# Gate and up products of two chunks as 2x2 blocks by Strassen's method in a fused attention and SwiGLU kernel

## The chip, the cores and the metric

The kernel runs on one core of a Trainium2 chip. The metric is the device time of one execution in microseconds (us), lower is better. Engines are named as in the profile: PE (TensorE, the matrix multiplier, with PEld for its weight loads), DVE (VectorE), ACT (ScalarE), POOL (GpSimd) and SP (SyncE, which here issues transfers and passes semaphores on). SBUF is the on-chip memory that all of them work from; PSUM is the memory in which matmuls accumulate, in 8 banks of 128 x 512 numbers.

## What is computed

Two branches read the same x (2048 rows of 640) and are mixed by a gate per row. Branch A is attention over 4 segments of 512 rows with 32 heads of 20 columns, and a linear memory that each segment reads and adds to. Branch B is a SwiGLU network with 1728 hidden columns:

```python
def _B_ref(x, w1, w3, w2):
    gate = jnp.einsum("bsd,df->bsf", x, w1)
    up = jnp.einsum("bsd,df->bsf", x, w3)
    h = _silu(gate) * up
    out = jnp.einsum("bsf,fd->bsd", h, w2)
    return out

x = A_x
g = _sigmoid((x * gate_w).sum(-1, keepdims=True))
a = _A_ref(x, A_wq, A_wk, A_wv, A_wo, A_beta)
b = _B_ref(x, B_w1, B_w3, B_w2)
return g * a + (1 - g) * b
```

The change is in `gate` and `up`, and in what stands around them.

## The kernel before

**Tiling.** A segment of 512 rows of x is a chunk; chunks 0 and 1 are pair A, chunks 2 and 3 pair B. x lies transposed: 128 of its 640 columns on the partitions, 512 rows along them, so a chunk is five such k-blocks (KB = 5). The 1728 hidden columns are 13 tiles j of 128 and a half tile of 64 (NF = 13 is the number of the half tile, in which gate and up share one weight tile). Every fp32 operand of a projection is kept as two fp32r parts, high and low (`split`, L177-184: ACT rounds the high part, DVE or POOL subtracts to get the low one), and every product is three passes: high by high, high by low, low by high (`PASSES`).

**Two halves of PE.** A matmul over 128 rows of the array is issued as two of 64 rows, one on the upper and one on the lower half (`halves`, L219). The two halves run at the same time. A piece of such work is a `Work`: its upper matmuls go first, then, one bank later in the stream, its lower ones, so that in the order of the program the lower half of one Work stands between the upper matmuls of the next. The lower half of a Work may begin when the upper one's last matmul has been signalled through an SP no-op (L272).

**gate and up.** For each j and each chunk of the pair there is one Work for the gate and one for up (`proj`, `ffn_up`): 15 products of 512 columns, as 30 matmuls of 64 rows. A pair has 4 Works and 120 matmuls per j. Each W tile is split once and used for both chunks. When the gate is in its bank, ACT takes tanh(g/2) (L1043), DVE makes (tanh+1)*g (L1040) and then 0.5*that*up (L1057); the tile is stored to DRAM (`hd`), from which `ffn_down` (the tiles f) reads it for the product with w2.

**Order.** Everything is written out by a planner in the program itself, which keeps a clock for each half of PE (`clocks`) and an end of work for each engine (`busy`), and writes the instructions of all engines in one order. The hardware executes that order, each engine its own rows in turn, with semaphores for what one engine needs of another. The stream of heavy Works (q, k, v, g, u, f, op) comes from segments `segs`; attention units (s: scores for the row maximum, t: scores for the exponentials, o: probabilities by v) are put in at fixed slots, `side` streams (`braid`) at fixed distances. When nothing heavy can go on the upper half, the planner writes lower ones (`lower`), else it moves its clock on (`force`). Tiles come from rings: NW weight tiles W, NRAW raw weight tiles, NFT tiles f, NHT tiles hT, 8 PSUM banks, two large slots `acc` for x raw, v and the output accumulators.

**Places.** The up stage of pair A runs from 125 to 366 us of the profiled execution (g and u with attention units between); that of pair B is spread between 590 and 930 us, with k, q, v and op work between.

Of the kernel before, what the change touches and what calls it, by code (L numbers as in the profile page):

```python
# [29 lines left out]
NFT = 6  # L30
NST, NW, NRAW, NHT, NVG, NB, FREE = 4, 9, 4, 4, 2, 8, 2000
# [20 lines left out]
def gated_mix(ctx: ExitStack, tc: tile.TileContext, xT, wqk, wv, w13, w2, w2h, wo, beta, out):  # L52
# [10 lines left out]
    hd = [dp.tile([4, 3, P, D], F32, name=f"hd{c}") for c in range(NSEG)]  # L63
# [122 lines left out]
    class Work:  # L186

        def __init__(self, name, parts, evac, old=None, olds=None, ready=None, hooks=None):
            self.ready, self.hooks = ready, hooks or {}
            self.name, self.parts, self.evac, self.old, self.olds = name, parts, evac, old, olds or {}  # L190
# [70 lines left out]
    def one(r, w):  # L261
# [6 lines left out]
        else:  # L268
            ins = nc.tensor.matmul(o, l, x, start=i == 0 and (r == 0 or not w.todo[0]),  # L269
# [58 lines left out]
    def events():  # L328
# [13 lines left out]
        for d in list(sides):  # L342
            if not d.on:
                sides.remove(d)
            elif dense["ns"] >= d.due and len(under) < 2 and len(behind_one) < 3:
# [4 lines left out]
                elif isinstance(y, Work) and (y.ready is not None and not y.ready() or not free(3) or busy["dve"] > now() + 2000):  # L350
# [6 lines left out]
    on_step, units = [], deque()  # L357
# [19 lines left out]
    def step(run):  # L377
# [82 lines left out]
    def slot(name):  # L460
        return cp.tile([P, 4 * H * VE], F32, tag="acc", name=name, bufs=2)
# [10 lines left out]
    def w_add(src, n, queue=nc.sync, needs=(), even=False, home=None):  # L472
        items.append((src, n, queue, needs, even, home))
        return len(items) - 1
# [21 lines left out]
    def w_load():  # L496
# [17 lines left out]
        clock["next"] += 1  # L514

    def w_split():
# [11 lines left out]

        def done():
            tiles[k] = w  # L530
            halfway.remove(k)
            if k not in EARLY:
# [4 lines left out]
    halfway, homes = set(), {}  # L537

    def w_step():
# [5 lines left out]
        elif raws and raws[0][0] < limit() and now() >= raws[0][3]:  # L545
# [6 lines left out]
    def w_get(i):  # L552

        while i not in tiles:
            if i >= limit():
                if not lower():
                    set_oldest(min(w.old for w in under if w.old is not None))
                    if i >= limit():
                        raise RuntimeError("no room for weight " + str(i))
# [6 lines left out]
            elif not raws or raws[-1][0] < i and len(raws) < NRAW:  # L566
# [208 lines left out]
    def q_block(c, mb, i, alloc, oldest=None, then=None):  # L775
# [7 lines left out]
        yield Work(f"q{c}_{mb}", proj(i, Xs[c]), evac, i if oldest is None else oldest, then and {3 * KB - 1: then})  # L783
# [76 lines left out]
    def v_blocks(c, iv, end):  # L860
# [3 lines left out]
        def begin_v():  # L864
            big["v", c] = V = slot(f"V{c}").rearrange("p (l h e) -> p l h e", l=4, e=VE)
# [915 lines left out]
```

## Time and profile before

| | |
|---|---|
| median of 3 runs | 1088.2 us (1087.52 to 1088.9) |
| the profiled execution | 1088.77 us, its span 1087.1 us |
| PE busy | 1073.8 us, 99% of the span, 11681 matmuls |
| DVE, ACT, POOL busy | 581.7, 483.5, 513.3 us (54%, 44%, 47%) |
| granted clock of PE | 0.998 of full speed |
| transfers | 184.36 MB, mean 170 GB/s |

The profile is one execution. A group row gives a line, an engine, an operation, the tiles written and read, the count, the busy time and the mean length of one instruction. The length of a matmul runs from its start until its result is through, so matmuls overlap and their lengths are not their spacing; spacing is read from the starts in the timeline. A busy share says only that some matmul is under way: with two halves of the array, PE is "busy" also when one half has nothing to do.

### The profile page before, as it was taken

What the parts mean: (1) busy time and instruction counts of PE and PEld (TensorE: products, weight loads), DVE (VectorE), ACT (ScalarE), POOL (GpSimd) and SP (SyncE); (2) the same over time, 40 slices, a digit from 0 to 9 for tenths busy, and PEclk for the clock granted to TensorE, in tenths of its full rate; (3) what the DMA queues carried; (4) which work ended last, traced back from release to release, by engine and by line L of the source; (5) the groups of instructions that cost most, each with busy time, mean ns of one, the idle gap of its engine ahead of it and who ended that gap; (6) DMA issues with size and microseconds to landing.
All of it is one profiled execution on the core that took longest, in us unless ns stands there. A gap on an engine that the chain in (4) does not pass through costs nothing.

```text
span 1087.1 us, 29863 instructions
## 1 busy us (share of the span) xinstructions
PE 1073.8 (99%) x11681; PEld 966.5 (89%) x11681; DVE 581.7 (54%) x1717; ACT 483.5 (44%) x1003; POOL 513.3 (47%) x718
## 2 busy tenths in 40 slices
PE   9999999999999999999999999999999999999998
PEld 7999998987877999899988889898888888899898
DVE  6022475444455676474544666774445665564553
ACT  6255324333333574353755653444333434565220
POOL 4543434353533446447564545647444543454250
PEclk9999999999999999999999999999999999999999
DMA  8465764444555555656776786655546463563541
GB/s 324 149 215 210 240 185 127 132 124 115 141 131 144 139 161 154 181 154 178 234 243 183 253 292 198 190 142 182 151 117 168 143 159 108 153 169 115 165 163 50
DMA packets 124645, 184.36 MB, mean 170 GB/s; under 512 B 21356, under 2 KB 65304, under 8 KB 124504
## 3 DMA queue, kind: packets, MB, share of 16 engines
q1 hardware_dynamic: 93064, 126.25, 37.1%
q0 software_dynamic: 23664, 42.04, 15.5%
q10 hardware_dynamic: 7776, 14.16, 3.5%
q8 instruction: 93, 1.52, 0.6%
q14 instruction: 48, 0.39, 0.1%
HBM read 112.23 MB, written 69.21 MB: 167 GB/s over the span
## 4 chain that ended last, share of the span: by engine, by line
PE 92%; DMA 3%; POOL 1%; issue 1%; DVE 1%; ACT 1%; SPq 0%; POOLq 0%; DVEq 0%
PE g L269 17%; PE f L269 17%; PE u L269 15%; PE k L269 7%; PE v L269 7%; PE op L269 6%; PE o L1275 6%; PE q L269 5%; PE s L1180 4%; PE t L1242 4%; PE q L806 1%; PE pm L269 1%; DMA qk<-qkd 1%; PE nd L269 1%; DMA qk<-mr 1%
## 5 line engine op out<-in xcount | busy, mean ns | idle before, releaser
L269 PE MATMUL g<-X,W 64*128 64x512 f32 x1680 | 377.1, 394 | 0.0
L269 PE MATMUL u<-X,W 64*128 64x512 f32 x1560 | 351.9, 394 | 0.0
L1191 DVE CUSTOM_DVE_ANT_0 junk<-s,mask 128x128 bf16<-128x128 f32 (+3 forms) x512 | 251.2, 491 | 161.7 <-PE s L1180 122.1
L179 POOL TENSOR_TENSOR W<-wr,W 128x640 fp32r<-128x640 f32 (+2 forms) x133 | 206.5, 1557 | 177.2 <-ACT W L184 165.7
L269 PEld LDWEIGHTS g<-X,W 64*128 64x128 f32 x1680 | 259.5, 185 | 16.1 <-issue 2.0
L1249 ACT ACTIVATE P<-t 128x384 f32<-128x384 f32 (+1 forms) x384 | 181.0, 525 | 179.9 <-PE t L1242 170.0
L269 PEld LDWEIGHTS u<-X,W 64*128 64x128 f32 x1560 | 244.4, 185 | 14.4 <-issue 1.2
L1258 POOL TENSOR_SCALAR_AFFINE_SELECT P<-P 128x256 f32<-128x256 f32 (+1 forms) x192 | 95.5, 504 | 263.6 <-ACT P L1249 237.7
L269 PE MATMUL f<-XW,W 64*128 64x320 f32 x1536 | 160.9, 310 | 3.6 <-SPq L272 3.6
L269 PEld LDWEIGHTS f<-XW,W 64*128 64x128 f32 x1536 | 153.8, 186 | 4.6 <-SPq L272 4.1
L184 ACT CAST W<-wr 128x640 fp32r<-128x640 f32 (+2 forms) x170 | 119.7, 719 | 54.8 <-PE u L269 19.3
L269 PE MATMUL f<-W,W 64*128 64x320 f32 x1056 | 138.6, 309 | 0.0
L269 PEld LDWEIGHTS f<-W,W 64*128 64x128 f32 x1056 | 118.8, 186 | 1.2 <-issue 1.0
L269 PE MATMUL k<-X,W 64*128 64x512 f32 x600 | 108.3, 398 | 0.0
L1180 PE MATMUL s<-qk 60*128 60x256 f32 (+2 forms) x512 | 91.0, 326 | 1.9 <-DMA qk<-qkd 1.8
L1242 PE MATMUL t<-qk 62*128 62x256 f32 (+2 forms) x512 | 88.2, 325 | 3.2 <-DMA qk<-mr 1.4
L269 PE MATMUL op<-W,oT 64*128 64x320 f32 x960 | 90.7, 308 | 0.0
L269 PE MATMUL v<-W,X 64*128 64x322 f32 (+2 forms) x948 | 89.2, 310 | 0.0
L269 PEld LDWEIGHTS k<-X,W 64*128 64x128 f32 x600 | 81.2, 185 | 6.2 <-issue 0.6
L269 PEld LDWEIGHTS op<-W,oT 64*128 64x128 f32 x960 | 85.8, 185 | 0.6 <-issue 0.4
L1201 POOL DMA_DIRECT2D qk<-mr x128 | 73.0, 572 | 28.1 <-DVE mr L1217 25.2
L269 PEld LDWEIGHTS v<-W,X 64*128 64x128 f32 (+1 forms) x948 | 84.8, 186 | 0.3 <-issue 0.2
(120 smaller groups left out, 1358.9 us busy)
## 6 DMA issues: line engine op xcount, KB each, us to landing
qk<-qkd POOLq DMA_DIRECT2D x128, 240.0 KB, 4.5
wr<-in_w_dram SPq DMA_DIRECT2D x80, 320.0 KB
hd<-ft SPq DMA_DIRECT2D x52, 256.0 KB
qkd<-qs SPq DMA_DIRECT2D x20, 512.0 KB
qkd<-ks SPq DMA_DIRECT2D x20, 512.0 KB
wr<-hd SPq DMA_DIRECT2D x32, 320.0 KB
od<-oq ACTq DMA_DIRECT2D x32, 256.0 KB
wr<-in_wo_dram SPq DMA_DIRECT2D x20, 320.0 KB
```

Source lines behind the costliest of these rows:

```text
L179: return lambda: e.tensor_sub(dst[:, 1], src, dst[:, 0].bitcast(F32))
L184: stages(bank, ("act", ns, lambda: nc.scalar.copy(dst[:, 0], src)), low, done=done)
L269: ins = nc.tensor.matmul(o, l, x, start=i == 0 and (r == 0 or not w.todo[0]), stop=i == len(todo) - 1 and (r == 1 or not w.todo[1]), skip_ ...
L806: nc.tensor.matmul(ps[m], ws[m][:, a, kb * P:(kb + 1) * P], Xs[c][:, b, kb, :], start=count[m] == 0, stop=count[m] == 14, skip_group_check ...
L1180: nc.tensor.matmul(ps[i][:, o:o + n], q[:, qb * P:(qb + 1) * P], k[:, :n], start=qb != 1, stop=qb != 0, skip_group_check=True)
L1191: nc.vector.tensor_tensor_reduce(out=junk[:, :n], in0=ps[i][:, o:o + n], in1=mask[:, L - n:], scale=1.0, scalar=-3.0e38, op0=ALU.add, op1= ...
L1201: nc.gpsimd.dma_start(dst, src)
L1242: nc.tensor.matmul(ps[i][:, o:o + L - q0], k[:, kb * P:(kb + 1) * P], q[:, q0:], start=kb != 2, stop=kb != 3, skip_group_check=True)
L1249: nc.scalar.activation(u["P"][:, i, o:o + n], ps[i][:, b:b + n], AF.Exp, scale=SCALE)
L1258: nc.gpsimd.affine_select(d, d, pattern=[[0, 2], [0, n], [1, P]], base=0, channel_multiplier=-1, compare_op=ALU.is_ge, fill=0.0)
L1275: nc.tensor.matmul(ps[32 * i:32 * i + 32, kb * P:], heads[2 * p + i]["v"][:, kb], pairs[p + i // 2]["P"][:, i % 2, o:o + n], start=kb == 0 ...
```

## The change

For each j the pair's gate and up are written as a 2x2 block product: rows are the two chunks, inner blocks are k-blocks (0, 1) and (2, 3), columns are gate and up. Seven block products replace eight (Winograd's form, with sums of x and sums of weights as operands); k-block 4 is done directly as before. Each block product is 2 k-blocks x 3 passes x 2 halves = 12 matmuls, so a j has 7 x 12 + 24 = 108 matmuls for 120.

- `make_sums` loads the two chunks' raw k-blocks 0 to 3 once more (8 loads of 256 KB a pair, tiles sx), makes four sums of each (DVE or POOL), and splits them into S tiles that lie in the `acc` slots, and into k-blocks 0 and 1 of the second chunk's X, which they overwrite.
- `mix` makes the sums of a j's two raw weight tiles: five subtractions on DVE or on POOL. A j has four W tiles (one of them 256 wide) for two. The ring of W goes from 9 to 8 tiles, that of f from 6 to 8, of hT from 4 to 3.
- `ffn_pair` replaces `ffn_up`. Its seven Works of a j are c1, c6, c7, c4 in one bank, z5, z3 in a second, w2 in a third. A later Work of a bank adds to what stands in it, after ACT or DVE has read it: c6 may begin when ACT has copied c1 to a tile (a), c7 when c6 is copied (b), c4 when c7 is copied (d), z3 when DVE has added z5 to d. Then follow adds of b and d on DVE, tanh on ACT, and two products on DVE or POOL. The Works of block j and block j-1 are interleaved: c1(j) c7(j-1) z5(j-1) w2(j) c6(j) c4(j-1) z3(j-1).
- The half tile has a Work of its own (`ffn_half`), once for each chunk. hidden tiles of a pair are stored in one transfer of 512 KB for two of 256 KB. The factor 0.5 moves to `cgate`.
- The segments are arranged anew: k, q of chunks 2 and 3 are no longer done together (7 more weight tiles of wqk), all of the second pair's up work comes after chunk 3's projections, and the ends of the segments move (slots 38, 70, 76, 105 of heads become 35, 61, 77, 104).
- Where no Work is ready and no event is due, the planner now lets its clock go on by a step in place of an error.

```diff
-NFT = 6
-NST, NW, NRAW, NHT, NVG, NB, FREE = 4, 9, 4, 4, 2, 8, 2000
+NFT = 8
+NST, NW, NRAW, NHT, NVG, NB, FREE = 4, 8, 4, 3, 2, 8, 2000
...
     def open_work(w):
-        w.bank = k = take_bank()
-        w.ps = pp.tile([P, L], F32, tag=f"b{k}", name=w.name, bufs=1)
+        w.more = bool(w.box)
+        if w.more:
+            w.bank, w.ps = w.box
+        else:
+            w.bank = k = take_bank()
+            w.ps = pp.tile([P, L], F32, tag=f"b{k}", name=w.name, bufs=1)
+            if w.box is not None:
+                w.box += [k, w.ps]
...
-                if not heap:
-                    raise RuntimeError("nothing makes " + waiting[0].name + " ready")
-                force()
+                if heap:
+                    force()
+                else:
...
+                    dense["ns"] += STEP
+                    clocks[:] = [c + STEP for c in clocks]
...
+    def mix(w, ri, rj, k, done):
...
+        def sums(v):
+            v.tensor_sub(ri[:, a], rj[:, a], ri[:, a])
+            v.tensor_sub(t, rj[:, b], ri[:, a])
+            v.tensor_sub(rj[:, a], rj[:, b], rj[:, a])
+            v.tensor_sub(ri[:, b], ri[:, b], t)
+            v.tensor_sub(ri[:, e], ri[:, e], rj[:, e])
+        stages(None, either(1650, 3200, sums), done=lambda: split(w[:, :, :2 * P], t, None, 300, done, spare=EVEN))
...
+            def run(v, x=x):
+                v.tensor_add(x[2], x[2], x[1])
+                v.tensor_sub(x[1], x[0], x[1])
+                v.tensor_sub(x[0], x[2], x[0])
+                v.tensor_sub(x[3], x[3], x[0])
+            stages(None, either(2500, 5100, run), done=left.clear)
...
+            return dict(
+                c1=lambda: work("c1", chain, [(wa, k, xs(x, k)) for k in range(2)], copy_to("a")),
+                w2=lambda: work("w2", w, [(wa, k, xs(x, k)) for k in (2, 3, 4)], evac_w, drop=wa),
+                c6=lambda: work("c6", chain, [(wd, k, ss(2, k)) for k in range(2)], copy_to("b"), ("a",), wd, (2,)),
+                c7=lambda: work("c7", chain, [(wb, k, ss(3, k)) for k in range(2)] + [(wb, 4, xs(y, 4))], copy_to("d"), ("b",), None, (3,)),
+                z5=lambda: work("z5", z, [(wc, k, ss(1, k)) for k in range(2)], evac_5, (), None, (1,)),
+                c4=lambda: work("c4", chain, [(wc, k, xs(y, k)) for k in (2, 3, 4)], evac_4, ("d",), wc),
+                z3=lambda: work("z3", z, [(wb, 2 + k, ss(4, k)) for k in range(2)] + [(wb, 4, xs(x, 4))], evac_3, ("5",), wb, (4,)))
+        for p in plan:
+            now_ = block(*p)
+            for n, b in (("c1", now_), ("c7", last), ("z5", last), ("w2", now_), ("c6", now_), ("c4", last), ("z3", last)):
+                if b is not None:
+                    yield b[n]()
+            last = now_
...
-    seg += [braid(chain(jobs_up(A, FIRST)), job_read(1), 3800, 11000)]
-    segs.append((H + LAG + 1, seg))
+    half = job_half(1)
+    up = job_pair(A)
+    seg = [braid(braid(chain(q + [half, up]), (0, make_sums(A)), 400, 0), job_read(1), 3800, 11000)]
+    segs.append((H + 3, seg))
...
-    ks = jobs_k_held(B)
-    seg += ks[:KSKIP] + [alternate(chain(ks[KSKIP:]), job_up(B, 0))]
-    segs.append((2 * H + 6, seg))
...
+    segs.append((2 * H - 3, seg))
+    ks = jobs_k((2,), range(2)) + job_q((2,), 2) + job_q2((2,), 3)
...
-    tail = [braid(chain([d1b, take(d2, 14)]), o1, 1400, 6000), o2, d2]
+    tail = [braid(chain([d1b, d2]), o1, 1400, 6000), o2]
```

In the order of the program the two rows of `gate` and `up` look like this at the start of pair A's up stage. On PE before, the gate Work g0_0 (upper half) stands between the lower matmuls of the q projection:

```order
L269 MATMUL g0_0_1871<-X0_104,W15_1039 128x512
L269 MATMUL q1_3_1780<-X1_106,W13_919 128x512
L269 MATMUL g0_0_1871<-X0_104,W15_1039 128x512
L269 MATMUL q1_3_1780<-X1_106,W13_919 128x512
L269 MATMUL g0_0_1871<-X0_104,W15_1039 128x512
L269 MATMUL q1_3_1780<-X1_106,W13_919 128x512
```

and now, on PE at the first block of pair A (g1_13 is the half tile of chunk 1, c10_0 the chain bank and w20_0 the bank of w2 of chunk pair 0, block 0; S0_0 is a tile of sums):

```order
L275 MATMUL g1_13_1894<-X1_104,W15_1054 128x512 x8
L275 MATMUL c10_0_1958<-X0_102,W16_1154 128x512 x4
L1390 MATMUL s1_1_0_2040<-qk1_89 128x384
L1390 MATMUL s1_1_1_2041<-qk1_89 128x384
L275 MATMUL c10_0_1958<-X0_102,W16_1154 128x512 x2
L275 MATMUL w20_0_1976<-X0_102,W16_1154 128x512 x4
L1390 MATMUL s1_2_0_2061<-qk1_89 128x512
L1390 MATMUL s1_2_1_2062<-qk1_89 128x512
L275 MATMUL w20_0_1976<-X0_102,W16_1154 128x512 x4
L275 MATMUL c10_0_1958<-S0_0_1799,W17_1327 128x512 x2
```

Where upper and lower alternated, the rows from g1_13 to w20_0 are all lower halves, 22 of them with only two s pairs between; the next upper one is c6, the last row, which reads S and adds to the bank of c1.

The second place is ACT in the middle of pair A's up stage. Before, exponentials P, casts of W and the tanh of a gate:

```order
L184 CAST W33_3272<-wr33_2877 128x640 [waits DMAHW4_49,PE_49]
L1280 COPY oq4_3325<-o4_3308 128x512 [waits DMAHW3_49,PE_49]
L716 DMA od0_76<-oq4_3325 128x512 [waits DMAHW6_49,Activation_49]
L1043 ACTIVATE ft0_5_3340<-g0_5_3182 128x512 [waits DMAHW5_49,PE_49]
L1249 ACTIVATE P6_3355<-t6_0_0_3356 128x512 [waits PE_49,Pool_49]
L1249 ACTIVATE P6_3355<-t6_0_1_3357 128x512 [waits PE_49]
L1249 ACTIVATE P6_3355<-t6_1_0_3412 128x384 [waits PE_49]
L1249 ACTIVATE P6_3355<-t6_1_1_3413 128x384 [waits PE_49]
L1043 ACTIVATE ft1_5_3455<-g1_5_3301 128x512 [waits PE_49]
```

and now, with the copies a and d (L1212) of blocks 8 and 7:

```order
L1459 ACTIVATE P8_3884<-t8_1_0_3946 128x384 [waits PE_49]
L1459 ACTIVATE P8_3884<-t8_1_1_3947 128x384 [waits PE_49]
L184 CAST W51_3969<-wr49_3544 128x640 [waits DMAHW0_49,Pool_49]
L1212 COPY a0_8_3990<-c10_8_3909 128x512 [waits PE_49]
L1459 ACTIVATE P8_3884<-t8_2_0_4012 128x384 [waits PE_49]
L1459 ACTIVATE P8_3884<-t8_2_1_4013 128x384 [waits PE_49]
L1212 COPY d0_7_4024<-c10_7_3660 128x512 [waits PE_49,Pool_49]
L184 CAST W52_4047<-wr52_3741 128x640 [waits DMAHW1_49]
L1459 ACTIVATE P9_4088<-t9_0_0_4089 128x512 [waits PE_49,Pool_49]
```

Each of the two copies stands behind a pair of exponentials, the first behind a cast of W as well; PE's Works c6 and c4 are behind these copies. Before, no later matmul stood behind a tanh of the up stage except through the bank it frees.

More of the change, by code (lines that the diff above doesn't have):

```diff
@@ L349, in events @@
                     sides.remove(d)
-                elif isinstance(y, Work) and (y.ready is not None and not y.ready() or not free(3) or busy["dve"] > now() + 2000):
+                elif isinstance(y, Work) and (y.ready is not None and not y.ready() or not free(2) or busy["dve"] > now() + 2000):
                     d.held = y
@@ L514, in w_load @@
         clock["next"] += 1
+        kind = items[k][6]
+        if kind is not None:
+            kind[1].append(raw)
+            if len(kind[1]) == 2:
+                for i in range(2):
+                    raws.append([k + 1 + i, kind[1][i], D, t + AGE])
+                clock["next"] += 2
     def w_split():
@@ L1138, in ffn_down @@
         for c, lb in hi:
-            if first and lb == 0:
-                accs[c] = slot(f"acc{c}")[:, :4 * D].rearrange("p (b d) -> p b d", b=4)
             for hf in range(2):
@@ L1391, in over @@
                 done()
-        while c not in turned:
+        while c not in turned or c == 1 and read.count(2) < 8:
             yield 1
```

298 lines of the change are left out of this document (215 added, 83 removed).

## Prediction

> **What bounds the kernel now.** I read the page first: engines, then the chain that ended last, then the costliest groups.
>
> ```profile
> PE 1073.8 (99%) x11681; PEld 966.5 (89%) x11681; DVE 581.7 (54%) x1717; ACT 483.5 (44%) x1003; POOL 513.3 (47%) x718
> ...
> PE 92%; DMA 3%; POOL 1%; issue 1%; DVE 1%; ACT 1%; SPq 0%; POOLq 0%; DVEq 0%
> ...
> L269 PE MATMUL g<-X,W 64*128 64x512 f32 x1680 | 377.1, 394 | 0.0
> L269 PE MATMUL u<-X,W 64*128 64x512 f32 x1560 | 351.9, 394 | 0.0
> ```
>
> PE is the bound: busy 99% of the span, 92% of the chain. So what counts is how long PE's rows take, and what PE waits for. The waits of PE alone, of which these are the longest, are small:
>
> ```profile
> PE f L269 <- SPq L272: 3.6, 2, 2.2
> PE s L1180 <- DMA qk<-qkd: 1.8, 3, 1.0
> PE t L1242 <- DMA qk<-mr: 1.4, 2, 1.0
> ```
>
> How long a row takes is seen in the timeline of PE, in three stretches: gate and up alternating on the two halves; f alternating; and the end of the kernel, where only one Work is left and its second half runs alone (start, length, matmuls).
>
> ```profile
> 204.06 0.39 PE L269 MATMUL u<-X,W 64*128 64x512 f32 x1
> 204.12 0.39 PE L269 MATMUL g<-X,W 64*128 64x512 f32 x1
> 204.29 0.39 PE L269 MATMUL u<-X,W 64*128 64x512 f32 x1
> 204.36 0.39 PE L269 MATMUL g<-X,W 64*128 64x512 f32 x1
> ...
> 393.45 3.48 PE L269 MATMUL f<-W,W 64*128 64x320 f32 x44
> ...
> 1081.51 1.93 PE L269 MATMUL f<-XW,W 64*128 64x320 f32 x12
> ```
>
> u and g start as good as together, and each comes again 0.23 us later. So a half takes a 512-wide matmul every 0.23 us, and two halves that both have work take one every 0.115. Of f (0.31 us long) 44 in a row span 3.48 us: (3.48-0.31)/43 = 0.074 each with both halves at work. The 12 at the end span 1.93 us: (1.93-0.31)/11 = 0.147 each, twice as much. **A matmul whose half works alone costs twice the PE time of a paired one**, and a busy share of 99% does not show it. That is the point on which this prediction turns.
>
> **The change part by part.**
>
> *Matmuls removed.* 12 of 120 for each of 13 j in two pairs: 12 x 26 = 312, as the program's order has it (3240 g and u become 2928). If all were paired, 312 x 0.115 = 35.9 us.
>
> *Pairing lost.* The planner pairs a Work's lower half with the next Work's upper half. g and u never waited for each other; the seven new Works do. c6 needs the copy of c1, c7 that of c6, c4 that of c7, z3 the add of z5, and each such copy comes only after the lower half of its Work is through. Where the next upper half may not begin yet, lower halves go alone: the 22 rows shown above are 21 such neighbours. A Work's rows are first all upper, then all lower ones, so neighbours on the same half can be counted in the order (the attention's own pairs left out). Before there are 422: 138 of 512 columns (q, k, g, u), 272 of 320 (v, f, op), 12 others. Now there are 773: 357, 405 and 11. In the new order c, w and z account for 214 of the 357; f and op grow by 117, with stages of their own now more often without a second Work beside them. Each such neighbour leaves the other half idle for one matmul: 0.230-0.115 = 0.115 us at 512, 0.147-0.074 = 0.073 at 320. In full: 219 more x 0.115 = 25.2, 133 more x 0.073 = 9.7, together 34.9 us. The lower end is 0, if the halves, which need not start together, caught up on each other. A doubled row in a short run can be made good by half a slot of offset, one in a long run can't. Neighbours in runs of five rows or more are 141 before and 425 now: 284 of the 351 more. I take these in full (284/351 x 34.9 = 28.2) and half of the rest (3.3): 31.5 us.
>
> *What the new Works wait for.* No row before shows a matmul that adds to a bank which another engine has just read. The nearest rows are the ACT copy of a bank and what stands before it in ACT's queue:
>
> ```profile
> L1280 ACT COPY oq<-o 128x512 f32<-128x512 f32 x32 | 18.8, 586 | 140.4 <-PE o L1275 136.4 <-DMA qk<-qkd 4.1
> L1249 ACT ACTIVATE P<-t 128x384 f32<-128x384 f32 x256 | 111.6, 490 | 108.3 <-PE t L1242 107.6
> L184 ACT CAST W<-wr 128x640 fp32r<-128x640 f32 x139 | 99.2, 730 | 47.2 <-PE u L269 19.3 <-DMA wr<-hd 9.6 <-DMA wr<-in_w2h_dram 7.0
> ```
>
> In the order, between the last matmul of c1 and the first of c6 stand some 24 others, with pairing 24 x 0.115 = 2.8 us; between c7 and c4 18 (2.1 us); z5 to z3 26 (3.0 us). A copy that finds ACT free takes 0.59 us; behind a pair of exponentials 0.59+2 x 0.49 = 1.57; behind a cast as well, 2.30. The first two are covered, the third is short by 0.2 at c4. Bounds: below, 0; above, all 104 such returns short by that 0.2 us, 21 us. Nothing makes a wait shorter than before, since PE's waits there were nil. I take 0 for the steady blocks, since the worst queue is barely longer than the cover, and 1 us for the first block of pair B: its sums lie in the slot of chunk 1's output and so stand behind that store (4.1 us to landing by the page's row for POOL's output stores), while only k3, the half tile, c1 and w2 are there to fill PE.
>
> ```profile
> out_dram<-acc POOLq DMA_DIRECT2D x8, 320.0 KB, 4.1
> ```
>
> *Other work added, off PE.* By stage A of before (125 to 366 us; PE, PEld, DVE, ACT, POOL busy):
>
> ```profile
> 125.00:366.00 241.00, 239.70 (x2275) 208.65 (x2273) 129.97 (x435) 89.04 (x188) 101.27 (x147) 1.00 0.50 139
> ...
> L1040 DVE SCALAR_TENSOR_TENSOR ft<-ft,g 128x512 f32<-128x512 f32 x52 | 35.6, 685 | 58.8 <-ACT ft L1043 58.8
> L1357 DVE TENSOR_TENSOR oall<-oall,rr 128x512 f32<-128x512 f32 x20 | 13.7, 684 | 7.2 <-PE rr L269 6.9
> L179 DVE TENSOR_TENSOR W<-wr,W 128x640 fp32r<-128x640 f32 x26 | 23.1, 894 | 5.1 <-ACT W L184 4.7 <-POOL P L1258 0.4
> L179 DVE TENSOR_TENSOR oT<-oall,oT 128x256 fp32r<-128x256 f32 x16 | 6.7, 421 | 2.4 <-ACT oT L184 2.3
> L606 DVE TENSOR_TENSOR W<-wr,W 128x128 fp32r<-128x128 f32 x2 | 0.5, 284 | 0.0
> ...
> L184 ACT CAST oT<-oall 128x256 fp32r<-128x256 f32 x16 | 6.5, 407 | 15.1 <-PE op L269 14.8 <-DVE oall L1382 0.3
> ...
> L179 POOL TENSOR_TENSOR W<-wr,W 128x640 fp32r<-128x640 f32 x113 | 177.9, 1580 | 149.3 <-ACT W L184 141.3 <-DVE oT L179 6.5 <-PE s L1180 0.2
> L179 POOL TENSOR_TENSOR W<-wr,W 128x512 fp32r<-128x512 f32 x10 | 12.9, 1289 | 7.8 <-ACT W L184 7.8
> ```
>
> DVE loses 52 products (35.6 us) and gets 13 x (3 adds + 2 products) x 0.685 = 44.5, 9 mixes x (4 x 0.421 + 0.284) = 17.7, 15 more low parts of W x 0.894 = 13.4, 4 of 256 columns = 1.7, 12 products with b and d x 0.69 = 8.3: 130.0-35.6+85.6 = 180 us in some 239, 75%. ACT gets 39 copies x 0.586 = 22.9, 15 casts x 0.73 = 11.0 and 13 narrow ones x 0.407 = 5.3: 89 to 128 us, 54%. POOL's rows give 2.27 ns a column, so some 0.71 us for 256 columns (an estimate from the two): 4 mixes of 3.2, 9 narrow low parts of 0.71 and 14 products of 1.29 are 37 us, 101 to 138, 58%. All of it lies beside PE and costs nothing as long as queues stay shorter than the cover above; without that cover, each late return costs what it is late. SP gets 78 more no-ops between halves, and one store a j for two; transfers grow by 16 x 256 KB for the sums and 9 x 320 KB of weights on a mean of 170 GB/s. No PE row waits for these; I cost them at nothing, and at most at the 3.6 us that PE f waited for SP before.
>
> *Sum.* Against the profiled execution, 1088.77 us (0.05% over the median): 1088.8 - 35.9 + 31.5 + 1 = 1085.4. A measurement here can tell about 0.2%, 2.2 us; so the forecast is faster by three tenths of a per cent, and close to no change.
>
> **The rivals.**
>
> *A. The saving arrives whole:* idle halves cost nothing because PE runs ahead elsewhere. For it: PE's busy share will be 99% either way. Against it: 0.147 for 0.074 in the last microseconds, and that nothing later can make up for PE time on a chain that is 92% PE. 1088.8-35.9+1 = 1054.
>
> *B. The returns come late (slower).* Place: c6, c7, c4 and z3 in 26 blocks, 104 returns, behind ACT and DVE in their order. For it: ACT's cover is 0.2 us short in the worst queue, DVE goes from 54% of stage A to 75%, and where a lower half already runs alone, the planner had nothing else to give PE. Against it: only a few returns have both exponentials and a cast in front. It decides from 0.06 us a return: then 104 x 0.06 = 6 us outweigh the net 3.4 and the 2.2. At 0.15 us, 15.6 us: 1101.
>
> *C. DVE and POOL shut each other out.* The rows for ops on SBUF operands (shortest, median, longest in ns) and one case:
>
> ```profile
> L179 DVE TENSOR_TENSOR W<-wr,W x37: 684/822/2020, 16.8 to 1034.8; 128x640 fp32r<-128x640 f32 x26, 128x512 fp32r<-128x512 f32 x6, 128x642 fp32r<-128x642 f32 x5
> ...
> 307.42 0.68 DVE L1040 SCALAR_TENSOR_TENSOR ft<-ft,g 128x512 f32<-128x512 f32 x1
> ...
> 322.56 1.05 DVE L179 TENSOR_TENSOR W<-wr,W 128x640 fp32r<-128x640 f32 x1
> ...
> 306.98 1.57 POOL L179 TENSOR_TENSOR W<-wr,W 128x640 fp32r<-128x640 f32 x1 [0.63 <-ACT W L184]
> ...
> 323.00 1.48 POOL L1258 TENSOR_SCALAR_AFFINE_SELECT P<-P 128x256 f32<-128x256 f32 x2
> ```
>
> A DVE op with one operand in PSUM kept its 0.68 us beside a POOL subtraction; the one with both in SBUF took 1.05 beside two POOL selects, and up to 2.02. The change puts some 91 ops with two SBUF operands on DVE in stage A (45 of mix, 21 low parts, 25 products) where there was one or two. If each waits w, DVE is full at 59/91 = 0.65 us. At 0.75, 9 us over in each stage: 1085+18 = 1103. The mean wait so far is 0.894-0.822 = 0.07. [...]
>
> *D. No change.* Net saving and new waits cancel: 3 us of waits make 1088.
>
> **How the numbers follow.** Forecast (1074 to 1086, faster) 0.42, with the pairing loss between 20 and 31.5. A 0.06 (1054). D 0.25 (1086 to 1091). B 0.22 (1091 to 1105). C 0.05 (1103). Faster by over 0.2%: 0.42+0.06 = 0.48; within 0.2%: 0.25; slower: 0.27. The range is 1074 to 1101: it leaves out A, C and the upper part of B. The forecast's own range is 1074 to 1086.
>
> **What would show it.** Right: PE still busy 98 to 99% with some 300 matmuls fewer; stretches of PE's timeline in which 512-wide matmuls of c, w and z start 0.23 us apart; a row of c6 that follows w2 after single lower halves. The first up stage, 241 us long, would be no shorter than by 5 us or so. B would show PE c waiting for ACT L1212, or z for DVE L1243, with several us in total; C, mixes on DVE well over 1.97 us; A, c, w and z spaced by 0.115 throughout. Wrong: a time under 1070 means that a half alone isn't the price I give it; over 1101, that the returns are later than ACT's rows allow.

## The result, and the profile after

The changed kernel takes 1123.7 us (median of 4 runs, 1122.9 to 1124.3) where the kernel before took 1088.6 beside it: ratio 1.032 (95% interval 1.030 to 1.034), some 35 us slower. The forecast was 1085.4 us, its range 1074 to 1101.

The profiled execution took 1123.7 us, its span is 1121.6 us, its granted clock 0.984 (before: 1087.1 and 0.998). The page's engine line and the shares of the chain:

```profile
PE 1083.7 (97%) x11369; PEld 963.2 (86%) x11369; DVE 728.8 (65%) x1929; ACT 562.3 (50%) x1158; POOL 611.1 (54%) x812
...
PE 81%; DMA 6%; DVE 5%; issue 2%; POOL 2%; SPq 2%; ACT 1%; DVEq 0%; ACTq 0%; POOLq 0%
```

There are 312 matmuls fewer, and PE is busy 10 us longer. Its share of the chain falls from 92% to 81%; transfers, DVE and POOL have taken the rest. PE idles for 1121.6-1083.7 = 37.9 us, where it was 13.3. Who made it wait, longest in total first, and PE's groups of the new Works with the idle time ahead of them:

```profile
PE t L1452 <- DMA qk<-mr: 10.1, 6, 3.4
PE f L275 <- SPq L278: 4.2, 2, 2.6
PE t L1452 <- ACT P L1459: 3.6, 1, 3.6
PE t L1452 <- DVE m L1401: 2.4, 2, 1.8
PE c L275 <- SPq L278: 1.9, 1, 1.9
PE rr L275 <- DVE ns L441: 1.8, 1, 1.8
```

```profile
L275 PE MATMUL c<-X,W 64*128 64x512 f32 x936 | 233.1, 400 | 2.4 <-SPq L278 1.9 <-DVE gm L895 0.5
L275 PE MATMUL c<-S,W 64*128 64x512 f32 x624 | 179.2, 400 | 0.0
L275 PE MATMUL z<-X,W 64*128 64x512 f32 x468 | 131.1, 398 | 0.0
```

The Works that wait for copies (c, z) show 2.4 us of idle time, none of it behind a copy (ACT L1212) or an add (DVE L1243). What waits is the attention: its unit t, for the row maxima (m, made on DVE from s, turned, and brought into qk by a DMA that POOL issues) or for ACT behind other work. t's three rows are 16.1 us, and PE idles 24.6 more than before. Next come waits for SP, which passes PE's signals between the halves on and issues transfers: all rows behind SP are 9.4 us together, where it was 3.6 before.

The second loss stands in the clock column of the page's windows (stretch, length, busy time of PE, PEld, DVE, ACT, POOL, granted clock, DMA share, GB/s). Before, every stretch of 100 us but one had 1.00 (0.98 from 400 to 500). After:

```profile
500.00:600.00 100.00, 92.30 (x1001) 83.54 (x1000) 49.53 (x155) 59.87 (x127) 59.70 (x83) 0.97 0.75 241
600.00:700.00 100.00, 96.92 (x1060) 83.70 (x1058) 69.97 (x207) 46.87 (x103) 60.28 (x93) 0.97 0.70 226
700.00:800.00 100.00, 93.94 (x748) 76.83 (x748) 80.35 (x202) 49.26 (x102) 51.47 (x67) 0.93 0.50 143
```

Six of the half-clock stretches lie right behind lulls of PE of 1.8 us or more; a seventh, 6.8 us from 659 us on, follows a lull of only 0.6. The clearest place is the start of pair B's up stage. First DVE, then POOL, SP and PE (start, length, and in brackets the idle time ahead and who ended it), then the windows:

```profile
712.62 1.94 DVE L1147 TENSOR_TENSOR sx<-sx,sx 128x512 f32<-128x512 f32 x1
...
719.94 2.62 DVE L578 TENSOR_TENSOR wr<-wr,mix 128x256 f32<-128x256 f32 x1
...
723.50 0.29 DVE L1401 CUSTOM_DVE_ANT_0 junk<-s,mask 128x128 bf16<-128x128 f32 x1
...
725.81 0.69 DVE L1092 TENSOR_TENSOR ft<-ft,g 64x512 f32<-64x512 f32 x1
```

```profile
720.28 1.29 POOL L179 TENSOR_TENSOR S<-sx,S 128x512 fp32r<-128x512 f32 x1
721.52 0.75 POOL L179 TENSOR_TENSOR W<-mix,W 128x256 fp32r<-128x256 f32 x1
```

```profile
726.53 1.29 SPq L766 DMA_DIRECT2D hd<-ft  x2
```

```profile
724.42 0.47 PE L1452 MATMUL t<-qk 62*128 62x512 f32 x1 [0.66 <-DVE m L1401]
...
727.93 1.64 PE L275 MATMUL c<-X,W 64*128 64x512 f32 x3 [1.90 <-SPq L278]
```

```profile
720.00:724.00 4.00, 3.76 (x27) 2.31 (x17) 3.90 (x7) 0.58 (x1) 3.28 (x5) 1.00 0.22 69
724.00:728.00 4.00, 1.69 (x8) 1.10 (x8) 3.76 (x11) 2.19 (x4) 0.00 (x0) 0.96 0.04 9
728.00:732.00 4.00, 4.00 (x12) 3.21 (x13) 2.23 (x5) 3.80 (x9) 1.70 (x2) 0.50 0.81 221
732.00:736.00 4.00, 4.00 (x15) 3.00 (x16) 2.15 (x5) 0.62 (x1) 0.00 (x0) 0.50 0.01 5
```

Sums of X (sx) and of weights (wr, mix) follow each other on DVE. The one of 2.62 us takes 0.42 at the median; beside it POOL subtracts on SBUF operands. The row maximum (junk) stands behind them, and PE waits 0.66 us. The second lull, 1.90 us, comes through SP: its signal for PE (L278) stands behind the store of the half tile (hd<-ft), which had waited for DVE's product ft, late as well. PE then has half its clock through two windows in which it is "busy" all the time.

The two longest lulls have other sources. Before the first, of 3.56 us up to 532.31, a cast of X on ACT waits for a load of raw x that takes 11.16 us, and the exponentials that t waits for stand behind that cast; DVE has nothing to do for 5.2 us there. From the chain:

```profile
519.31 11.16 DMA xr<-in_xT_dram
...
530.49 0.63 ACT X L437
```

Before the second, of 3.40 us, DVE has the row maxima ready (mr) by 565.2, but POOL issues their transfer only at 569.81, behind subtractions, masks and other issues; it lands at 576.9, over 6 us later, where the median of these transfers is 3.6:

```profile
564.39 0.84 DVE L1427 STREAM_TRANSPOSE mr<-ns 32x32 f32<-32x32 f32 x4
```

```profile
563.78 3.11 POOL L179 TENSOR_TENSOR W<-wr,W 128x642 fp32r<-128x642 f32 x2
...
569.81 1.12 POOL L1411 DMA_DIRECT2D qk<-mr  x2
```

```profile
576.98 0.59 PE L1452 MATMUL t<-qk 62*128 62x512 f32 x2 [3.40 <-DMA qk<-mr]
```

**An account of the time.** From the page and the clock: idle is span minus PE's busy time; half clock is (1 - granted clock) x span; the rest is PE at work. Before: 13.3, 2.2 and 1071.6. After: 37.9, 17.9 and 1065.8. So the rest fell by 5.8, idle rose by 24.6 and half clock by 15.7, together the 34.5 us of the spans. The prediction's matmuls and pairing were to give -35.9 + 31.5 = -4.4. The same account for every run below (us against before), each from its one profiled execution; these spans lie up to 4.5 us from the runs' medians, so a difference of a few us between two rows tells little:

| run | idle | half clock | rest | rest by the order |
|---|---|---|---|---|
| changed kernel | +24.6 | +15.7 | -5.8 | -0.5 |
| 312 matmuls left out of before | -1.3 | -0.1 | -31.8 | -34.3 |
| new order, eight products | +5.4 | +4.4 | +7.3 | +7.0 |
| own banks | +23.4 | +8.9 | -11.9 | -12.1 |
| no sums of weights | +17.0 | +13.3 | -10.9 | -3.7 |
| no sums of X | +17.1 | +12.2 | -6.8 | -2.4 |
| neither | +15.7 | +4.4 | -7.4 | -4.6 |
| sums to POOL | +26.7 | +19.3 | -4.1 | +1.4 |
| pair A only | +2.4 | -1.1 | -6.8 | -9.9 |
| pair A only, sums to POOL | +11.9 | +5.5 | -7.8 | -7.6 |
| lulls in before | +32.3 | +14.8 | +1.0 | 0 |
| DVE load in before | +18.4 | +10.2 | +14.3 | +3.9 |
| the same as reciprocals | +7.9 | +8.9 | +7.8 | +3.9 |

The last column is worked out from PE's order alone at the prediction's prices: matmuls left out x 0.115, more same-half neighbours x 0.115 (512 columns) or 0.073 (320), all in full. It follows the rest within 4 us in eight of the thirteen, and stands 4 to 7 us too high in four with the method's many short Works; that some doubled rows are made good there is a guess. Only with the DVE load of subtractions the rest rose by 10 more than the order says, though PE's order is the same as with the reciprocals; why is open. (The prediction gives the changed kernel 357 and 405 neighbours, the expectation of the run with own banks 329 and 341: two ways of counting, whose sums against before differ by half a microsecond, -1.0 and -0.5.)

### The profile page after: what moved, and what is told of

The parts are those of the page before. It is cut to its first block, busy times and chain, and to the rows that moved or that the text cites. A ratio compares the mean times of both kernels' runs of the same rounds, so it can differ in the third digit from the quotient of the medians.

```text
span 1121.6 us, 29797 instructions
## 1 busy us (share of the span) xinstructions
PE 1083.7 (97%) x11369; PEld 963.2 (86%) x11369; DVE 728.8 (65%) x1929; ACT 562.3 (50%) x1158; POOL 611.1 (54%) x812
## 4 chain that ended last, share of the span: by engine, by line
PE 81%; DMA 6%; DVE 5%; issue 2%; POOL 2%; SPq 2%; ACT 1%; DVEq 0%; ACTq 0%; POOLq 0%
PE f L275 17%; PE c L275 15%; PE z L275 7%; PE op L275 6%; PE v L275 5%; PE o L1485 5%; PE k L275 5%; PE q L275 4%; PE w L275 4%; PE t L1452 3%; PE s L1390 3%; DMA qk<-mr 3%; DVE junk L1401 2%; DMA xr<-in_xT_dram 2%; PE q L857 1%
## 5 line engine op out<-in xcount | busy, mean ns | idle before, releaser
L275 PE MATMUL c<-X,W 64*128 64x512 f32 x936 | 233.1, 400 | 2.4 <-SPq L278 1.9
L275 PE MATMUL c<-S,W 64*128 64x512 f32 x624 | 179.2, 400 | 0.0
L184 ACT CAST W<-wr 128x640 fp32r<-128x640 f32 (+2 forms) x205 | 144.5, 722 | 53.8 <-PE f L275 20.2
L275 PEld LDWEIGHTS c<-X,W 64*128 64x128 f32 x936 | 153.6, 188 | 13.5 <-SPq L278 2.6
L275 PE MATMUL z<-X,W 64*128 64x512 f32 x468 | 131.1, 398 | 0.0
L275 PE MATMUL w<-X,W 64*128 64x512 f32 x468 | 130.7, 398 | 0.3 <-SPq L278 0.3
L275 PEld LDWEIGHTS c<-S,W 64*128 64x128 f32 x624 | 115.1, 188 | 7.8 <-issue 0.6
L1452 PE MATMUL t<-qk 62*128 62x256 f32 (+2 forms) x512 | 103.4, 333 | 16.4 <-DMA qk<-mr 10.1
L275 PE MATMUL v<-W,X 64*128 64x320 f32 (+2 forms) x948 | 95.0, 313 | 0.6 <-SPq L278 0.6
L275 PEld LDWEIGHTS w<-X,W 64*128 64x128 f32 x468 | 86.0, 187 | 6.4 <-SPq L278 0.7
```

What stands on the lines that cost most here:

```text
L184: stages(bank, ("act", ns, lambda: nc.scalar.copy(dst[:, 0], src)), low, done=done)
L275: ins = nc.tensor.matmul(o, l, x, start=not w.more and i == 0 and (r == 0 or not w.todo[0]), stop=i == len(todo) - 1 and (r == 1 or not w. ...
L1452: nc.tensor.matmul(ps[i][:, o:o + L - q0], k[:, kb * P:(kb + 1) * P], q[:, q0:], start=kb != 2, stop=kb != 3, skip_group_check=True)
```

## The experiments

**Theory after the result:** the terms for matmuls and pairing were right; lost is what the prediction put at nothing, lulls of PE behind late side work, and the half clock behind the lulls. Rivals: the new order of segments makes the lulls; the returns or the pairing cost more than counted.

(Of each edit the parts that matter are shown, some of them within a line.)

**Matmuls left out, pairing kept** (on the kernel before):

```diff
-proj(idx[k], Xs[c])
+proj(idx[k], Xs[c], range(2, KB) if k and c == cs[1] else range(KB))
```

> The kernel before with 12 of the 120 matmuls of each j left out (the products of u of the second chunk with k-blocks 0 and 1), so 312 fewer, everything else as before; u of chunks 1 and 3 is then not the reference's. Theory: the matmul term of the prediction holds where the pairing stays, 312 x 0.115 = 35.9 us, so 1052 to 1057 us. Rival: the attention's chain, not the number of matmuls, sets the pace, and the gaps left on PE are not filled: above 1075 us.

1056.3 us, ratio 0.970 (0.968 to 0.971). With its pairs kept, a matmul less is worth its price: -33 of 35.9 us, idle and clock as before. The attention does not set the pace.

**The new order alone** (on the changed kernel):

```diff
-        plan = [(j, plan_pair(j)) for j in range(NF)]
+        plan = [[w_add(w13[2 * j], D), w_add(w13[2 * j + 1], D)] for j in range(NF)]
...
+                    yield from ffn_up(cs, j, plan[j], j == NF - 1)
```

> The changed kernel with the eight conventional products back in both pairs (g and u, no sums of X, no sums of weights, no adds of c, z and w), in the changed kernel's order of segments, tiles and slots. Theory (the new order makes the stalls): PE's waits between 416 and 783 us and the half-clock windows behind them stay, and 106 more same-half neighbours of 320 columns than before cost 106 x 0.073 = 8 us: 1115 to 1135 us. Rival (Strassen's own work on DVE and POOL, or its returns, make the stalls): only the 8 us remain, 1090 to 1100 us.

1105.3 us, ratio 1.015 (1.013 to 1.016): between the two. 7 us are the neighbours of f and op, 9.8 are lulls and half clock. Its longest waits:

```profile
PE t L1487 <- DMA qk<-mr: 4.4, 4, 2.0
PE op L275 <- DVE oT L179: 3.5, 1, 3.5
PE f L275 <- SPq L278: 2.6, 1, 2.6
```

So the order has a quarter of the 40 us of idle and half clock; thirty come with the method itself.

**Own banks** (on the changed kernel): `needs` empty for c6, c7, c4 and z3, no shared box, each bank freed by its own copy or add.

```diff
-copy_to("b"), ("a",), wd, (2,)),
+copy_to("b"), (), wd, (2,)),
```

> The changed kernel with a bank of its own for each of the seven products of a j, so that none waits for a copy of an earlier one; the values of c6, c7, c4 and z3 are then not the sums that the method needs. Same-half neighbours in PE's order fall from 329 to 212 at 512 columns and rise from 341 to 363 at 320: 117 x 0.115 - 22 x 0.073 = 12 us less. Theory (pairing is paid at its price, the rest of the loss is stalls that don't come from the returns): 1108 to 1116 us. Rival (the returns themselves are late, or lost pairing costs more than counted): under 1100 us.

1113.9 us, ratio 1.022 (1.019 to 1.025), within the theory's range. No Work waits for a copy's value any more, and idle time stays 23.4 over before; one wait of 3.3 us, of z, is now for a bank that a copy frees. Late returns are out as the main cause, the more so as no row of the changed kernel waits for one. The pairing's price is borne out in part only: PE's own work falls by 6.1 of the 12 us, and 6.8 us of the shorter span are half clock.

**No sums of weights** (on the changed kernel):

```diff
-        stages(None, either(1650, 3200, sums), done=lambda: split(w[:, :, :2 * P], t, None, 300, done, spare=EVEN))
+        split(w[:, :, :2 * P], ri[:, a], None, 300, done, spare=EVEN)
```

> The changed kernel without the five subtractions of weight tiles in each j (the raw tiles go into the split as they are), which leaves out the sums of weights. DVE and POOL lose about 26 x 2 us of operations with two SBUF operands. Rival C (DVE and POOL shut each other out and so delay the attention's row maxima): PE's waits go down by half or more and the time falls by 15 us or more, under 1108 us. Theory of the order: the waits between 416 and 600 us stand where no weight is mixed; only 33 fewer 512-wide same-half neighbours, 4 us: 1117 to 1124 us.

1105.4 us, ratio 1.014 (1.012 to 1.016): 18 us less than the changed kernel. By the spans it is 15: idle time 7.6, half clock 2.4, the rest 5.1 with its 33 neighbours. The time speaks for the load, though idle time fell by a third of what it had risen by, not by half.

**No sums of X** (on the changed kernel):

```diff
-            stages(None, either(2500, 5100, run), done=left.clear)
-            while left or not free_slots():
+            while not free_slots():
```

> The changed kernel without the adds and subtractions of make_sums (the raw k-blocks of X are split as they are), which leaves out the sums of X; loads, splits and everything else stay. Theory (the sums of pair B at 700 us stand in DVE's queue ahead of row maxima): the lulls at 723 to 728 us and the 10.2 us at half clock behind them go, 5 + 3 us or so: 1112 to 1118 us. Rival (weights' sums and the order make that stall): within 4 us of the changed kernel.

1111.9 us, ratio 1.021 (1.019 to 1.022), 12 us less. The lulls at 723 and 726 us are one of 1.8 at 721, the 10.2 us of half clock behind them 3.4. At that place this is some 4 of the 12 us (0.8 of lulls, 3.4 of half clock), and the lull that is left waits for a copy of the new Works (ACT b L1205). Where the other 8 us come from was not taken apart.

**Neither sum:**

> The changed kernel with neither the sums of weights nor those of X (both left out at once; the adds of c, z and w stay). Theory (what DVE and POOL have more to do makes the stalls, and the two parts add up): 18 us without the sums of weights and 12 without those of X, 1123.7 - 30 = 1094, so 1090 to 1098 us; idle time and half clock of PE together come down to what the new order has alone, some 25 us. Rival (the two relieve the same stalls, and copies and adds of c, z and w hold the rest): above 1101 us.

1105.5 us, ratio 1.015 (1.012 to 1.019): the rival. By the medians the two parts don't add up: 18 us together, no more than the sums of weights alone. (By the profiled spans it is 22 of 27; this run's four times spread over 7 us, and the profiled one is the shortest.) The half clock comes down to that of the new order alone, the idle time to 29.0 only. Its longest waits are now f and q behind SP (4.0, 3.6) and rr behind DVE (2.4). So the loss of 35 us has three parts by the medians: 16 us by the new order, about nothing by the method without its sums (it saves 15 us of PE's own work and loses 10 in idle time), and 18 by the sums. What makes the 10 us of idle time that are left over the new order's 18.7 (the copies and adds of c, z and w, the extra casts, the order that the planner then writes) was not taken apart.

**DVE loaded in the kernel before**, with nothing of the method in it:

```diff
+            t = sp.tile([P, L], BF, tag="junk", name="junk", bufs=1)
+            nc.vector.tensor_sub(t.rearrange("p (a b) -> p a b", a=16), wide, wide)
...
+        for k in range(4):
+            later(now() + 900 * k, sub)
```

> The kernel before with four more subtractions of 512 columns with SBUF operands on DVE behind each u, whose results nobody reads: 208 x 0.69 = 143 us more on DVE, about what the changed kernel has more (147). Theory (side work on DVE in front of the attention's row maxima makes PE wait): PE's idle time goes up by 10 us or more and half-clock windows follow, 1100 to 1118 us. Rival (the stalls hang on the order and the places of the changed kernel, not on DVE's load): within 4 us of before, under 1093 us.

1130.4 us, ratio 1.036 (1.034 to 1.038): DVE work that no one reads costs more than the whole change. It is more than expected, 39 us. The group of the load and POOL's largest, then the same two where the load is reciprocals with one SBUF operand:

```profile
L87 DVE TENSOR_TENSOR junk<-small 128x512 bf16<-128x512 f32 x208 | 174.7, 840 | 5.0
...
L192 POOL TENSOR_TENSOR W<-wr,W 128x640 fp32r<-128x640 f32 x115 | 184.7, 1611 | 176.0 <-ACT W L197 162.1 <-DVE acc L1140 7.0 <-DMA wr<-in_wo_dram 5.4
```

```diff
-            nc.vector.tensor_sub(t.rearrange("p (a b) -> p a b", a=16), wide, wide)
+            nc.vector.reciprocal(small, small)
```

> The kernel before with the same four extra operations on DVE behind each u, now as reciprocals of 128x112 with one SBUF operand, in place of subtractions with two (by the row 128x128 at 950 ns some 0.84 us each, as long as the subtractions took on the mean, 840 ns). Theory 1 (DVE's occupancy alone delays the row maxima): the same loss as with the subtractions, 1122 to 1135 us. Theory 2 (what hurts is that DVE's and POOL's operations on SBUF wait for each other): POOL's subtractions come back from 1611 to 1580 ns and the time is under 1110 us.

```profile
L85 DVE RECIPROCAL small<-small 128x112 f32<-128x112 f32 x208 | 176.7, 849 | 3.4
...
L190 POOL TENSOR_TENSOR W<-wr,W 128x640 fp32r<-128x640 f32 x115 | 180.6, 1575 | 175.8 <-ACT W L195 163.2 <-DVE acc L1138 6.3 <-PE f L280 4.7
```

1115.9 us, ratio 1.024 (1.023 to 1.025), between the two theories. The same 175 us on DVE, at the same order of PE, cost 26 us as reciprocals, with POOL's row at 1575 ns (1580 before), and 39 as subtractions, with POOL's at 1611. So the larger part needs no longer rows on POOL. DVE's queue does get slower: from the end of an s matmul to the start of its row maximum on DVE (512 of each, taken in order from the timeline) it is 0.75 us on the mean before, 1.41 with the reciprocals, 1.69 with the subtractions, and 1.11 in the changed kernel. Yet this mean does not rank the losses: with 1.41 PE idles 7.9 us more than before, with 1.11 in the changed kernel 24.6. And the place counts. The reciprocals keep DVE as busy in pair A's up stage (100 to 400 us) as in pair B's (700 to 1000), but PE's busy time stays within 0.2 us of before in the first and falls by 7.7 in the second, where the clock falls too:

```profile
100.00:400.00 300.00, 298.53 (x2942) 263.94 (x2941) 232.82 (x613) 122.11 (x251) 128.97 (x190) 1.00 0.55 150
...
700.00:1000.00 300.00, 289.29 (x2896) 257.46 (x2895) 226.41 (x615) 124.26 (x262) 147.94 (x211) 0.97 0.52 141
```

What makes pair B's stage so much more sensitive was not tested.

**Work shifted from DVE to POOL** (on the changed kernel, and on the pair A kernel below):

```diff
-max(busy["dve"], now()) + dve < max(busy["pool"], now()) + pool
+max(busy["dve"], now()) + dve + 4000 < max(busy["pool"], now()) + pool
```

> The changed kernel with its choice between DVE and POOL (sums of weights, sums of X, last products) shifted to POOL: DVE only where POOL would end more than 4 us later. All is computed. Theory (DVE is the queue that delays): DVE's busy time falls by 40 us or more and the time by 8 us or more, under 1116 us, although 14 more same-half neighbours cost 2 us. Rival (POOL's queue issues the row maxima's transfers and delays them as much): 1124 us or more.

> Pair A by seven products, pair B by eight, in the old order, with the choice between DVE and POOL shifted to POOL as in the run on the changed kernel. Theory (DVE is the queue that delays): a little faster than pair A alone, 0.994 of the time before or less. Rival (POOL delays as much, and 25 more same-half neighbours of 512 columns cost 2.9 us): 0.996 to 1.000.

1126.9 us, ratio 1.034 (1.030 to 1.038), and 1098.7 us, ratio 1.008 (1.007 to 1.010): the rival in the first; the second is slower than even the rival said. On the changed kernel DVE is 43 us less busy (685.3) and POOL 70 more (680.8). Row maxima start 0.90 us behind their matmuls in place of 1.11, but PE waits as long for their transfer, and for more of what POOL does:

```profile
PE t L1452 <- DMA qk<-mr: 12.4, 8, 2.4
...
PE s L1390 <- DMA qk<-qkd: 3.3, 4, 1.7
PE o L1485 <- POOL P L1468: 3.0, 2, 2.6
```

POOL masks P and issues the loads of qk; the attention is no earlier when the work stands there. It isn't one engine's queue.

**Lulls in the kernel before:**

```diff
+            if kb == 1 and p % 6 == 4:
+                for _ in range(1 + p // 2 % 2):
+                    ins = lull = order(nc.sync.dma_start(still, xT[0, :, 0, :16]), ins)
```

> The kernel before with ten lulls put into PE's order: in the middle of ten products of P by v, PE waits for one small transfer (five times) or for two in a row (five times) that is issued behind the matmul in front. Everything is still computed. Theory (a lull of 2 us or so is followed by a stretch at half clock): 5 x 2 + 5 x 4 us of idle time and up to ten windows of 3.4 us at half clock, 17 us: 1125 to 1140 us, a granted clock of 0.98 to 0.985. Rival (the half-clock windows of the changed kernel come from something else, such as its load): the clock stays at 0.998 and the time is 1110 to 1120 us.

1135.5 us, ratio 1.040 (1.038 to 1.042), clock 0.985. The ten lulls have 30.4 us together, and half clock came with 14.8 more. PE's waits, then the windows around one lull of 3.53 us (306.6 to 310.2):

```profile
PE o L1277 <- DMA still<-in_xT_dram: 30.4, 10, 4.2
```

```profile
304.00:308.00 4.00, 2.63 (x26) 0.95 (x23) 1.46 (x8) 0.00 (x0) 0.22 (x1) 1.00 0.71 159
308.00:312.00 4.00, 1.84 (x18) 1.00 (x20) 0.00 (x0) 0.27 (x1) 0.00 (x0) 0.62 0.02 2
312.00:316.00 4.00, 4.00 (x22) 3.07 (x22) 0.00 (x0) 0.85 (x3) 0.00 (x0) 0.53 0.17 66
```

All six lulls of 3.5 to 4.2 us in this run were followed by half clock (3.4 or 6.8 us); of six between 1.5 and 2.4 us, two were. So a lull in this run cost its length and then up to half of 3.4 or 6.8 us more.

**Pair A only**, in the old order from chunk 2 on: the eight products (`ffn_up`) for pair B, and the segments of the kernel before from `ks = jobs_k_held(B)` to the tail.

> Pair A's gate and up by the changed kernel's seven products, pair B's by the conventional eight, and from chunk 2's k on the order of segments of the kernel before. 156 matmuls fewer than before, 156 x 0.115 = 17.9 us; 62 more same-half neighbours of 512 columns and 11 more of 320, 62 x 0.115 + 11 x 0.073 = 7.9 us; idle time of PE in the up stage as in the changed kernel, some 2 us more than before. Theory (what was lost came from the new order and from pair B's stage): 17.9 - 7.9 - 2 = 8 us less than before, 1078 to 1084 us. Rival (the method's own side work makes stalls in any order): 1088 us or more.

1084.6 us, ratio 0.994 (0.992 to 0.996): a little faster than both kernels. Its engine line, and the costliest wait of an attention unit:

```profile
PE 1065.9 (99%) x11525; PEld 956.5 (88%) x11525; DVE 660.1 (61%) x1831; ACT 522.0 (48%) x1077; POOL 550.2 (51%) x751
```

```profile
PE t L1487 <- DMA qk<-mr: 2.8, 5, 1.3
```

In pair A's stage the same side work makes hardly a lull and no half clock (over the whole kernel 2.4 us more idle time, clock 0.999). Half the method, without the new order and without pair B's sums among k, q and attention, keeps 6 of the 18 us that its 156 matmuls are worth.

## Why the prediction was wrong

- **PE is the bound, and a half alone costs double: right.** Just before the first c6, eight lower halves of g alone take (2.02-0.39)/7 = 0.233 us each, as was told from other rows:

```profile
134.68 2.02 PE L275 MATMUL g<-X,W 64*128 64x512 f32 x8
136.53 0.40 PE L275 MATMUL c<-X,W 64*128 64x512 f32 x1
```

- **Matmuls -35.9, pairing +31.5: right.** PE's own work fell by 5.8 where 4.4 were forecast. With 312 matmuls left out and the pairs kept it fell by 31.8, so the pairing cost some 26 us, a little less than forecast (that half of the doubled rows in short runs cost nothing was the author's estimate, which no run took apart); the run with own banks got 6 of its 12 us back in PE's own work.
- **What the new Works wait for, nothing in the steady blocks: right.** No c or z row waits for a copy or an add. The 1 us at pair B's first block was too small and for the wrong reason: it was not the store of chunk 1 but sums on DVE, ahead of row maxima and of the half tile's product that SP waited for: 0.66 + 1.90 us of lulls and 10.2 us at half clock.
- **"All of it lies beside PE and costs nothing as long as queues stay shorter than the cover above": this step failed.** It was worked out for stage A and carried over to the rest of the kernel, and it held the side work against the returns alone. In stage A it came true: DVE's load was 191 us where 180 were forecast (the third busy time of the window), 79% of the stage, and PE idled 2.3 us, 1.3 before, at full clock. From 400 us on it did not: between 400 and 1000 us PE is busy 20 us less than before, and all the half clock lies there or at the end. What the runs showed in its place is 24.6 us of idle time and 15.7 of half clock, of which the new order alone has 9.8, and 18 us less time without the sums. What is late is the attention, whose row maxima go through DVE, POOL and a DMA, and its exponentials through ACT; a late transfer and the queues of POOL, ACT and SP held it as well as DVE's. "No PE row waits for these" was wrong of SP and the transfers: the rows behind SP grew from 3.6 us to 9.4, and the longest lull is behind a load of x. The load put into the kernel before shows a loss without the method: 26 us where DVE is only occupied (4 of them by the order of PE), 39 where POOL's subtractions take longer as well (1611 ns for 1575).

```profile
125.00:366.00 241.00, 238.67 (x2239) 205.45 (x2237) 191.05 (x528) 130.20 (x265) 146.03 (x187) 1.00 0.55 156
```

- **The new order, counted through its neighbours only:** they were right (7 us measured with the eight products), but it brings 9.8 us of lulls and half clock that had no term.
- **Rival C was nearest in kind, and its threshold was wrong.** It let DVE and POOL exclude each other, to 1103 us, from 0.65 us a wait, where DVE would be full. Last products on DVE (H by d and b) took 1152 and 1097 ns on the mean where an addition of the same width with an operand in PSUM took 684, so 0.4 to 0.5 us more; low parts of W took 982. The sign named for C came only faintly: the five rows of a mix on DVE add to 2.31 us by their means and to 1.97 by their medians, so most took no longer than forecast. DVE was never full (80.35 us in its fullest stretch of 100), and PE waited all the same. In the loaded kernel DVE's subtractions with two SBUF operands took 840 ns on the mean, where 690 were reckoned, and POOL's subtractions 1611 beside them (1580 before); beside DVE's reciprocals with one SBUF operand POOL's took 1575. The run with the subtractions lost 13 us more than the 26 of the reciprocals; how much of the 13 comes from the longer rows was not shown.

```profile
L179 DVE TENSOR_TENSOR W<-wr,W 128x640 fp32r<-128x640 f32 x59 | 57.7, 982 | 9.9 <-ACT W L184 8.8 <-POOL P L1468 0.9
...
L1229 DVE TENSOR_TENSOR H<-H,d 128x512 f32<-128x512 f32 x17 | 19.6, 1152 | 0.1
...
L1243 DVE TENSOR_TENSOR d<-d,z 128x512 f32<-128x512 f32 x26 | 17.8, 684 | 7.5 <-PE z L275 6.1 <-ACT P L1459 1.2
```

- **Rivals A, B and D are out:** A by the pairing that was paid, B by PE's waits, none of which is for a copy or an add, and by the own banks, D by the time.
- **The clock had no term.** 15.7 us. Its stretches of half clock in the changed kernel are 3.4, 6.8 and 10.2 us long; the lulls put into the kernel before took its clock from 0.998 to 0.985. Lulls shorter than the shortest stretch had half clock behind them as well: of 1.8 to 2.6 us (1.97 in the run with lulls; 2.57, 1.79 and 2.37 in the changed kernel), and once in the changed kernel one of 0.6.

Shown by runs: the prices of matmuls and lulls, that returns are not the main cause, that load on DVE makes a loss of this size without the method, and that leaving out the sums of weights and of X takes 18 and 12 us off, both 18. Argued from single places of the trace: through which queue each lull came. Open: what holds the 10 us of idle time that stay without both sums, why pair B's stage is hit and pair A's hardly, and how much of the POOL side is issue of transfers and how much masks.

## What to carry to other kernels

Before costing work on an engine with spare time at nothing, look for the latency chain that runs through its queue, and ask what PE's next unit has to wait for if each link gets half a microsecond longer. A busy share does not answer it: 79% on DVE cost next to nothing in pair A's up stage (PE idled 2.3 us, 1.3 before), and the two longest lulls came between 500 and 600 us, where DVE was 50% busy. So look at every stage that gets more work, not at one. Price a stall of PE at its length plus the half clock behind it (here 14.8 us behind the 30.4 of ten lulls). And where matmuls are saved at the price of dependent, shorter pieces, count the pairs of halves in the order first: the count gave the right sum here (-4.4 us forecast with the matmuls, -5.8 measured).

## What was not expected of the hardware

- Half clock after lulls of 1.8 to 2.6 us (though not after every one: after two of six between 1.5 and 2.4 us in the run with lulls), in stretches of 3.4, 6.8 and 10.2 us, and of 13.7 us in the run with reciprocals (from 721 us, around lulls of 2.90 and 1.78).
- A DVE operation of four columns took 6.31 us once, where the shortest took 0.23. During the longest, from 622.37 to 628.68 us, POOL makes four subtractions back to back, the last up to 628.65. The row gives shortest, median and longest ns:

```profile
L954 DVE TENSOR_SCALAR gate<-gate x4: 232/1374/6307, 42.3 to 622.4; 128x4 f32<-128x4 f32 x4
```

- A reciprocal of 128x112 takes as long (849 ns) as a subtraction of 128x512 in the loaded kernel (840), and leaves POOL's subtractions at 1575 ns where the other made them 1611.
